# w_out turned by the host, the straight w_out narrowed in later blocks, and another order of the opening

## The chip, the cores and the metric

The kernel runs on one core of a Trainium2 chip. The metric is the device time of one execution in microseconds (us); lower is better. Engine names are those of the profile: PE multiplies matrices, PEld loads its weights, DVE and ACT do element-wise work, POOL is the general engine, SP issues loads and stores. Lines (L348) are those of the kernel before; in the change most lines stand some 60 to 85 further down, and its order rows carry its own numbers.

## The reference

```python
# 1. chunked attention: 4 x 8 heads, 768 tokens, head_dim 64; a chunk of 32 queries sees 56 keys and 8 memory keys
scores = scale * q_c @ k_full.T
a = exp(scores - max); a = a / (sum(a) + 1e-9); x = a @ v_full      # -> x (3072, 512)
# 2. a rational layer, w_in (512, 2048), w_out (2048, 512)
h = x @ w_in
g = (a0 + a1*h + a2*h**2 + a3*h**3) / (1 + |b0|*|h| + |b1|*h**2 + 1e-6)
x2 = g @ w_out
# 3. soft mixture: phi (512, 32), 8 experts of 4 slots, w1 (8, 512, 1024), w2 (8, 1024, 512)
logits = x2 @ phi
d = softmax over the tokens; c = softmax over the slots
slots = d.T @ x2;  y = relu(slots @ w1) @ w2 per expert;  out = c @ y
```

The weights w_in and w_out come as float64 (the draw makes them so); all else is float32.

## The kernel before

x2 is never formed. The logits are g @ (w_out @ phi): the 2048 x 32 product w_out @ phi is made once, in 16 tiles `wp`, and slots is (d.T @ g) @ w_out, with w_out needed as rows only at the very end.

The 3072 tokens are taken in 6 **blocks** of 512, and a block in 8 **steps** of 256 columns of h, 48 steps kk = 0 to 47. In a step PE makes h (`h_part`, L348), ACT and DVE the rational function (`run_step`: ACT L578, L579 and L581, then DVE L580, L590 and L591; ACT L595 and L596; POOL L556; DVE L603 and L604), PE turns the result (L374), and ACT copies it out of PSUM (L375). L578, which reads h, is the first operation of a step on ACT and is used below as its mark. Two h tiles exist in PSUM (`ps_h`); one comes free when L591 of its step has read it. Attention for two pairs of 128-token tiles of the next block runs between the steps, a slice at a time (`attention`, `slice_`). Block 0 multiplies in float32 with 8 matmuls a step; the later blocks use a split of x and w_in in two parts with 24 faster ones (`split_w`).

Float64 is narrowed on the chip (`f64_narrow`): a chunk of 128 x 1024 values comes as pairs of 32-bit words, and

```python
ACT.activation(lo, lo, AF.Copy, scale=LOW)                                   # L299
DVE.tensor_scalar(f, f, -F64_HI, F64_HI, ALU.max, ALU.min)                   # L300
ACT.activation(f, f, AF.Prelu, scale=2.0 ** -112, alpha=-(2.0 ** 32))        # L301
DVE.scalar_tensor_tensor(dst, hi, 3, lo, ALU.logical_shift_left, ALU.bitwise_or)   # L303
```

make 1024 float32 a row of it. There are 8 chunks of w_in (loads "i0" to "i7", L312) and 8 of w_out ("o0" to "o7", L317), all narrowed in the opening and in block 0, since block 0 uses a new chunk of w_in in every step and needs `wp` in its products with the logits. For a chunk of w_out, `narrow_w_out` also stores the float32 rows to a DRAM buffer `wo_dr` (POOL, L335), from where they come back at the end; `wp_chunk` turns them on PE (8 transposes, L447) and copies the two halves out, one on ACT (L451), one on DVE (L449); `wp_sum` multiplies by phi (L457, L462) and copies `wp` (L459, L463). The staging pool `p_g` has four buffers.

The order comes from the strings of `KN`. "loads" is the order of the first loads on SP: q, k and v of a pair of token tiles (q is 0.5 MB, k, v and a weight chunk 1 MB each), "c" the constants (three small loads, L266 to L268). "pre" orders the opening: A and B are the attention of the first two pairs of tiles, s, n and t narrow i0, o0 and i1, "f" are matmuls that only keep PE at work (`busy`, L284). "ord0", "ord" and "ordl" order a step of block 0, of blocks 1 to 4 and of block 5. In the opening the order on each engine is fixed by hand, but a scheduler may still put instructions of the part behind it between those; so the queue of an engine must be read, not the strings. The queues are served in order.

## Time and profile before

| what | us |
|---|---|
| median of 3 runs (582.21 to 582.49) | 582.41 |
| the profiled execution, device time | 583.87 |
| its span, first to last instruction | 582.1 |
| PE busy | 542.7 |
| DVE busy | 447.2 |
| ACT busy | 415.4 |
| POOL busy | 121.4 |

The profiled execution is 1.46 us above the median, and 1.8 us of it lie outside the span. Busy times are averages over stages that differ: the opening (0 to 39.84 us, where L578 first starts) is full of loads, block 0 lasts from there to 135.5 us, blocks 1 to 5 to about 500 us, and then come the experts with 32 MB of w1 and w2. Each stage is read by itself below.

### The profile page before, as it was taken

How to read it: one execution, taken by the hardware profiler on the slowest of the kernel's cores; microseconds unless marked ns; L12 is line 12 of the kernel's file. 1: busy time of each engine (PE TensorE's matmuls, PEld its weight loads, DVE VectorE, ACT ScalarE, POOL GpSimd, SP SyncE). 2: the span in 40 equal slices, each digit the busy share in tenths (PEclk: the TensorE clock that was granted, in tenths of full speed). 3: DMA queues.
4: the chain of work that ended last, by engine and by line, in shares of the span. 5: the costliest groups of instructions: out<-in, count | busy, mean ns of one | idle time of the engine just before them, and what ended most of it. 6: DMA issues, size and time to landing. Idle time of an engine off the chain costs nothing.

```text
span 582.1 us, 13606 instructions
## 1 busy us (share of the span) xinstructions
PE 542.7 (93%) x5910; PEld 369.7 (64%) x5910; DVE 447.2 (77%) x567; ACT 415.4 (71%) x542; POOL 121.4 (21%) x64
## 2 busy tenths in 40 slices
PE   6699999999999999999999999999999999899981
PEld 5554455457767777677766777767778577447351
DVE  4769999979998989878798798896987868821042
ACT  1489999888978878768887686877787869520132
POOL 0010322213221331313132222222132233100000
PEclk9799999999999999999999999999999999999996
DMA  8889874401135303231032111320374423989939
GB/s 354 353 333 384 306 258 193 144 37 48 62 110 182 110 7 103 75 110 73 2 109 74 62 59 64 109 75 1 109 272 163 144 78 142 393 309 377 411 138 358
DMA packets 21371, 97.41 MB, mean 167 GB/s; under 512 B 2624, under 2 KB 2752, under 8 KB 16320
## 3 DMA queue, kind: packets, MB, share of 16 engines
q1 hardware_dynamic: 20160, 92.35, 43.1%
q0 software_dynamic: 1152, 4.19, 1.8%
q8 instruction: 46, 0.75, 0.5%
q14 instruction: 13, 0.11, 0.1%
HBM read 86.05 MB, written 10.49 MB: 166 GB/s over the span
## 4 chain that ended last, share of the span: by engine, by line
PE 55%; DVE 14%; ACT 13%; DMA 9%; issue 3%; POOL 2%; SPq 0%; ACTq 0%; POOLq 0%; DVEq 0%
PE h L348 30%; PE m L374 5%; PE m L427 4%; PE lg L367 3%; ACT S L578 3%; DMA win<-in_moe_w_dram 3%; ACT S L579 3%; POOL S L556 2%; PE m L224 2%; DMA g<-in_moe_w_in_dram 2%; DMA g<-in_moe_w_out_dram 2%; DVE T L591 2%; ACT g L375 2%; DMA T<-in_moe_w_dram 2%; DVE S L580 2%
## 5 line engine op out<-in xcount | busy, mean ns | idle before, releaser
L348 PE MATMUL h<-xt,win 128*128 128x512 f32 x1024 | 269.9, 411 | 1.5 <-ACT xt L246 0.6
L348 PEld LDWEIGHTS h<-xt,win 128*128 128x128 f32 x1024 | 185.7, 188 | 48.1 <-issue 9.3
L556 POOL TENSOR_TENSOR S<-S,S 128x1024 f32<-128x1024 f32 x46 | 111.5, 2423 | 298.5 <-DVE S L580 298.5
L578 ACT ACTIVATE S<-h,ctab 128x1024 f32<-128x1024 f32 x47 | 52.4, 1114 | 50.2 <-PE h L348 48.9
L580 DVE SCALAR_TENSOR_TENSOR S<-S,S 128x1024 f32<-128x1024 f32 x47 | 57.4, 1222 | 37.6 <-ACT S L579 37.3
L590 DVE TENSOR_TENSOR T<-T,h 128x1024 f32<-128x1024 f32 x47 | 57.0, 1213 | 6.8 <-ACT T L581 6.6
L374 PEld LDWEIGHTS m<-ident,T 128*128 128x128 f32 x384 | 43.0, 141 | 29.5 <-issue 15.9
L591 DVE SCALAR_TENSOR_TENSOR T<-T,ctab,h 128x1024 f32<-128x1024 f32 x47 | 59.9, 1274 | 0.8
L603 DVE SCALAR_TENSOR_TENSOR T<-T,ctab,S 128x1024 f32<-128x1024 f32 x46 | 58.6, 1274 | 0.0
L604 DVE SCALAR_TENSOR_TENSOR T<-S,T 128x1024 f32<-128x1024 f32 x46 | 56.2, 1221 | 2.2
L581 ACT ACTIVATE T<-h,ctab 128x1024 f32<-128x1024 f32 x47 | 57.5, 1223 | 0.0
L375 ACT ACTIVATE g<-m 128x512 f32<-128x512 f32 x96 | 53.3, 601 | 3.2 <-PE m L374 2.9
L596 ACT ACTIVATE S<-S,ctab 128x1024 f32<-128x1024 f32 x47 | 54.4, 1158 | 0.9
L374 PE MATMUL m<-ident,T 128*128 128x128 f32 x384 | 52.6, 276 | 2.4 <-DVE a L185 1.4
L595 ACT ACTIVATE S<-S 128x1024 f32<-128x1024 f32 x47 | 50.4, 1073 | 6.0 <-DVE S L580 3.3
L579 ACT ACTIVATE S<-h,ctab 128x1024 f32<-128x1024 f32 x47 | 52.7, 1120 | 0.6 <-DVE T L603 0.6
L367 PE MATMUL lg<-T,wp 128*32 128x512 f32 x192 | 32.7, 605 | 1.3 <-DVE T L604 0.7
L348 PE MATMUL h<-xt,x 128*128 128x512 f32 x64 | 31.8, 608 | 0.0
L186 ACT ACTIVATE a<-a 128x512 f32<-128x512 f32 x22 | 13.6, 634 | 18.5 <-DVE a L185 18.5
L427 PE MATMUL m<-g,s 128*32 128x512 f32 x192 | 21.8, 595 | 0.4 <-ACT s L419 0.4
L335 POOL DMA_DIRECT2D wo<-win x8 | 5.8, 721 | 76.7 <-DVE win L303 67.9
L301 ACT ACTIVATE g<-g 128x1024 f32<-128x1024 f32 x16 | 18.6, 1173 | 3.0 <-DVE g L300 3.0
(193 smaller groups left out, 658.0 us busy)
## 6 DMA issues: line engine op xcount, KB each, us to landing
win<-in_moe_w_dram SPq DMA_DIRECT2D x32, 512.0 KB, 5.8
k<-in_kw_dram SPq DMA_DIRECT2D x11, 1024.0 KB, 8.0
v<-in_vw_dram SPq DMA_DIRECT2D x11, 1024.0 KB, 5.4
g<-in_moe_w_in_dram SPq DMA_DIRECT2D x8, 1024.0 KB, 7.6
g<-in_moe_w_out_dram SPq DMA_DIRECT2D x8, 1024.0 KB, 8.0
out_dram<-win SPq DMA_DIRECT2D x12, 512.0 KB, 5.0
q<-in_qw_dram SPq DMA_DIRECT2D x11, 512.0 KB, 3.6
wo<-win POOLq DMA_DIRECT2D x8, 512.0 KB, 7.0
```

The source lines that it names most:

```text
L348: PE.matmul(tile_[:, f2, :], lhsT=ww[:, c, f2 * P:f2 * P + P], rhs=xx[:, c, :], start=(n == 0), stop=(n == len(pairs) * NC - 1))
L374: st["turn"] = PE.transpose(pb[:, m, f2 * P:f2 * P + P], t_[:, f2, tt * P:tt * P + P], ident)
L375: ACT.activation(gts[b, qd][:, 2 * part:2 * part + 2, 2 * P * o:2 * P * o + 2 * P], pb, AF.Copy)
L556: POOL.tensor_tensor(out, q, w, ALU.mult)
L578: ACT.activation(s, hh, AF.Abs, scale=b0)
L579: ACT.activation(y, hh, AF.Square, scale=rb1)
L580: DVE.scalar_tensor_tensor(s, y, QC, s, ALU.add, ALU.add)
L581: ACT.activation(t, hh, AF.Identity, bias=a2, scale=a3)
L590: DVE.tensor_tensor(t, t, hh, ALU.mult)
L591: behind[kk] = DVE.scalar_tensor_tensor(t, t, a1, hh, ALU.add, ALU.mult).ins
L603: DVE.scalar_tensor_tensor(t, t, a0, w, ALU.add, ALU.mult)
L604: DVE.scalar_tensor_tensor(t, e, 2.0, t, ALU.subtract, ALU.mult, reverse0=True)
```

## The change

Five things change.

1. The host gives w_out a second time, turned (`w_turned`, float64, 8 chunks of 1 MB). Block 0 loads and narrows these in place of the straight ones ("o" and "n"), and `wp_sum` takes them as they are: `wp_chunk` with its transposes and copies is gone, and so are the stores to `wo_dr` in block 0.
2. The straight w_out is loaded and narrowed chunk by chunk in blocks 1 to 4 (`load_rows`, `narrow_rows`, "r" in "ord"): one chunk every three steps, from kk = 12 to 36, each with the four operations above and the store to `wo_dr`. Their buffers are the pool `p_x`, now 2 x 2048 in place of 4 x 1024 words a row.
3. The opening's attention takes each token tile by itself (`attention_first`), and the first h tile is made in two halves of 256 tokens, one after each pair (`h_first`; "H" and "J" are its two parts for pair 0 and pair 1).
4. The matmuls of `busy` are 512 columns long in place of 128, and there are 6 of them in place of 23.
5. The three loads of constants become one of 134 words a row, and the order strings are new. In a step of block 0, w_out is narrowed one chunk ahead in place of two.

```diff
-    'loads': "q0 q1 v0 i0 v1 c0 o0 i1 o1 q2 v2".split(),
-    'pre': "f10 A A f5 B B A A A A B B A A B B A A A A s B B B B A A f2 A B B A s A B B A f2 B s B B B c f4 n t n t t".split(),
-    'pre2': "i2 w0 z0 o2 n1 i3".split(),
-    'ord0': "at a1 w1 s2 h0 d1 at t o3 z1 i4 n2 at a2 y h1 p0 at p1 at at".split(),
-    'ord': "at a1 h0 d1 at t a2 y x2 h1 p0 p1 x1 at x3 at at".split(),
+    'loads': "q0 q1 v0 i0 v1 i1 c0 o0 q2 o1 v2".split(),
+    'pre': "f4 A A A A f2 A B A B B B A B B A A s B A A s A A A A H B B t t n B B n B B B B H J J c".split(),
+    'pre2': "i2 o2 i3".split(),
+    'ord0': "at a1 z0 s2 h0 d1 at t o3 i4 n1 at a2 y h1 p0 at p1 at at".split(),
+    'ord': "at a1 h0 d1 at t a2 y r x2 h1 p0 p1 x1 at x3 at at".split(),
...
+    def h_first(pair):
+        if 0 not in hs:
+            hs[0] = ps_h("h", [P, 2, BLK])
+        o = slice(P // 2 * pair, P // 2 * pair + P // 2)
+        x = xt[0][0].rearrange("p c (t r) -> p c t r", t=TT)
+        for f2 in range(2):
+            to = hs[0][:, f2, :].rearrange("p (t r) -> p t r", t=TT)
+            for c in range(NC):
+                PE.matmul(to[:, :, o], lhsT=w_f[0][:, c, f2 * P:f2 * P + P], rhs=x[:, c, :, o],
+                          start=(c == 0), stop=(c == NC - 1))
             yield
...
-        SP.dma_start(out=ctab[:, 0:4], in_=ca.unsqueeze(0).to_broadcast([P, 4]))
-        SP.dma_start(out=ctab[:, 4:6], in_=cb.unsqueeze(0).to_broadcast([P, 2]))
-        SP.dma_start(out=u_acc[:, 0:NC * NSLOT], in_=phi)
+        SP.dma_start(out=u_all[:, BLK - NC * NSLOT:BLK + 6], in_=cst)
...
-            PE.matmul(t, lhsT=ident, rhs=ident, start=True, stop=True)
+            PE.matmul(t, lhsT=ident, rhs=ident.unsqueeze(1).to_broadcast([P, 4, P]), start=True, stop=True)
...
-    def narrow_w_out(i):
-        f = scratch[i % 3].rearrange("p (j d) -> p j d", j=2)
-        yield from f64_narrow(f.bitcast(U32), stage_out.pop(i))
-        POOL.dma_start(out=wo_dr[i], in_=f)
-        wo[i] = f
+    def narrow_w_turned(i):
+        wos[i] = scratch[i % 3].rearrange("p (c f) -> p c f", c=NC)
+        yield from f64_narrow(wos[i].bitcast(U32), stage_out.pop(i))
+
+    def load_rows(i):
+        rows_of[i] = p_x("x", [P, 2, DM, 2], U32)
+        SP.dma_start(out=rows_of[i].rearrange("p c f w -> p c (f w)"), in_=w_out[i])
+
+    def narrow_rows(i):
+        src = rows_of.pop(i)
+        lo, hi = src[:, :, :, 0], src[:, :, :, 1]
+        ACT.activation(lo, lo, AF.Copy, scale=LOW)
+        f = hi.bitcast(F32)
+        DVE.tensor_scalar(f, f, -F64_HI, F64_HI, ALU.max, ALU.min)
+        yield
+        ACT.activation(f, f, AF.Prelu, scale=2.0 ** -112, alpha=-(2.0 ** 32))
+        t = p_x("x", [P, 2048])[:, 0:1024].rearrange("p (j d) -> p j d", j=2)
+        DVE.scalar_tensor_tensor(t.bitcast(U32), hi, 3, lo, ALU.logical_shift_left, ALU.bitwise_or)
+        POOL.dma_start(out=wo_dr[i], in_=t)
+        yield
...
-    def wp_chunk(i):
-        t = wo.pop(i)
-        ws = wos[i] = p_S("S", [P, 2, NC, P])
-        for j in range(2):
-            pb = bank([P, NC, P])
-            for c in range(NC):
-                PE.transpose(pb[:, c, :], t[:, j, c * P:c * P + P], ident)
-            if j:
-                DVE.tensor_copy(ws[:, j], pb)
-            else:
-                ACT.activation(ws[:, j], pb, AF.Copy)
...
+        elif what == "r":
+            n, m = divmod(kk - NSTEP - 4, 3)
+            if m != 1 and 0 <= n <= NSTEP:
+                with tc.issue_after(st["exp"]):
+                    if m == 2 and n < NSTEP:
+                        st["rows"] = narrow_rows(n)
+                        next(st["rows"])
+                    if m == 0 and n > 0:
+                        next(st["rows"])
+                    if m == 0 and n < NSTEP:
+                        load_rows(n)
```

How the queues stand at three places, with the program's own names. First SP, the ninth to the seventeenth load of the program. Before (g_163 is i1, g_161 and g_165 are o0 and o1, g_585 is i2; ctab and u take the constants):

```order
L266 DMA ctab_108<-in_moe_a_dram 128x4
L267 DMA ctab_108<-in_moe_b_dram 128x2
L268 DMA u_110<-in_moe_phi_dram 128x128
L317 DMA g_161<-in_moe_w_out_dram 128x2048
L312 DMA g_163<-in_moe_w_in_dram 128x2048
L317 DMA g_165<-in_moe_w_out_dram 128x2048
L128 DMA q_167<-in_qw_dram 128x1024
L129 DMA k_168<-in_kw_dram 128x2048
L135 DMA v_171<-in_vw_dram 128x2048
L312 DMA g_585<-in_moe_w_in_dram 128x2048
```

and now (g_157 is i1, g_160 and g_166 are the turned o0 and o1, g_560 is i2):

```order
L374 DMA g_157<-in_moe_w_in_dram 128x2048
L330 DMA u_109<-in_cst_dram 128x134
L379 DMA g_160<-in_w_turned_dram 128x2048
L128 DMA q_162<-in_qw_dram 128x1024
L129 DMA k_163<-in_kw_dram 128x2048
L379 DMA g_166<-in_w_turned_dram 128x2048
L135 DMA v_168<-in_vw_dram 128x2048
L374 DMA g_560<-in_moe_w_in_dram 128x2048
```

Before o1 now stand q and k of the third pair, and one load of constants in place of three.

Second ACT, around the copies of the transposed attention output into xt, which the first h waits for. Before (L246; m_541 and m_547 are those of pair 1, L299 and L301 the two ACT operations of a narrowing, L451 the copy of a turned w_out half, L578 the first operation of step 0):

```order
L246 ACTIVATE xt_143<-m_529 128x16x32
L299 ACTIVATE g_165<-g_165 128x1024
L246 ACTIVATE xt_143<-m_541 128x16x32
L246 ACTIVATE xt_143<-m_547 128x16x32
L271 ACTIVATE ctab_108<-ctab_108 128x2
L301 ACTIVATE g_165<-g_165 128x1024
```

and now (L297 is the copy into xt, m_528 and m_534 are pair 1; L361 and L363 the narrowing; L646 is what L578 was):

```order
L363 ACTIVATE g_157<-g_157 128x1024
L361 ACTIVATE g_160<-g_160 128x1024
L361 ACTIVATE g_166<-g_166 128x1024
L363 ACTIVATE g_160<-g_160 128x1024
L363 ACTIVATE g_166<-g_166 128x1024
L297 ACTIVATE xt_142<-m_528 128x16x32
L297 ACTIVATE xt_142<-m_534 128x16x32
L333 ACTIVATE u_109<-u_109 128x2
L336 ACTIVATE u_109<-u_109 128x1
L337 ACTIVATE u_109<-u_109 128x1
L361 ACTIVATE g_560<-g_560 128x1024
L363 ACTIVATE g_560<-g_560 128x1024
L646 ACTIVATE S_602<-h_446,u_109 128x1024
```

The copies of pair 1 stood behind one operation on o1; now they stand behind both, and behind the second one on o0. The narrowing of i2 now stands ahead of step 0.

Third ACT in blocks 1 to 4, between steps 17 and 18. Before (S_2562 is step 17, S_2695 step 18; L375 copies turned results, L383 the logits):

```order
L581 ACTIVATE T_2563<-h_2469,ctab_108 128x1024
L595 ACTIVATE S_2592<-S_2562 128x1024
L596 ACTIVATE S_2592<-S_2592,ctab_108 128x1024
L578 ACTIVATE S_2695<-h_2569,ctab_108 128x1024
L375 ACTIVATE g_2534<-m_2611 128x2x256
L375 ACTIVATE g_2534<-m_2617 128x2x256
L383 ACTIVATE s_11_2623<-lg_1981 128x512
```

and now (S_2434 is step 17, S_2569 step 18; L663 and L664 are what L595 and L596 were, L646 is L578, L457 is L375, L465 is L383, and L411 is the new first operation on a chunk of rows):

```order
L663 ACTIVATE S_2464<-S_2434 128x1024
L664 ACTIVATE S_2464<-S_2464,u_109 128x1024
L411 ACTIVATE x_2268<-x_2268 128x1024
L457 ACTIVATE g_2406<-m_2485 128x2x256
L457 ACTIVATE g_2406<-m_2491 128x2x256
L465 ACTIVATE s_11_2497<-lg_1843 128x512
L646 ACTIVATE S_2569<-h_2441,u_109 128x1024
```

The first operation of step 18 moved behind L411 and, here, behind three copies that followed it before. On DVE the clamp L413 of the same chunk and, in the next step, L417 stand between the operations of a step.

## Rows read from the trace of the kernel before

**Rows 1.** the page: busy us, share, instructions of each engine.

```profile
PE 542.7 (93%) x5910; PEld 369.7 (64%) x5910; DVE 447.2 (77%) x567; ACT 415.4 (71%) x542; POOL 121.4 (21%) x64
```

**Rows 2.** stretches: length, busy PE PEld DVE ACT POOL, PEclk, DMA share, GB/s.

```profile
0.00:39.84 39.84, 28.55 (x615) 22.33 (x616) 22.32 (x54) 17.57 (x26) 1.46 (x8) 0.91 0.87 344
39.84:135.50 95.66, 90.76 (x898) 49.01 (x897) 88.26 (x103) 87.13 (x112) 22.52 (x14) 1.00 0.59 216
...
174.10:412.20 238.10, 234.88 (x2818) 172.21 (x2817) 203.86 (x246) 185.49 (x237) 60.17 (x25) 1.00 0.24 80
```

**Rows 3.** the chain that ended last, up to 55 us: start, length, what.

```profile
3.06 13.62 DMA g<-in_moe_w_in_dram
...
16.70 12.81 DMA g<-in_moe_w_out_dram
...
29.53 1.20 ACT g L299
30.73 0.97 ACT xt L246 x2
...
31.74 7.13 PE h L348 x16
```

**Rows 4.** timeline of ACT, to 42 us: start, length, instruction [idle before <-releaser].

```profile
29.53 1.20 ACT L299 ACTIVATE g<-g 128x1024 uint32<-128x1024 uint32 x1 [0.58 <-DMA g<-in_moe_w_out_dram]
30.62 1.06 ACT L246 ACTIVATE xt<-m 128x512 f32<-128x512 f32 x2
...
39.34 0.60 ACT L451 ACTIVATE S<-m 128x512 f32<-128x512 f32 x1 [1.70 <-PE m L447]
39.84 1.11 ACT L578 ACTIVATE S<-h,ctab 128x1024 f32<-128x1024 f32 x1
```

**Rows 5.** the page: DMA issues, KB each, median us from issue to landing.

```profile
k<-in_kw_dram SPq DMA_DIRECT2D x11, 1024.0 KB, 8.0
...
q<-in_qw_dram SPq DMA_DIRECT2D x11, 512.0 KB, 3.6
```

**Rows 6.** stretches again, 16 to 22 us.

```profile
16.00:18.00 2.00, 0.79 (x56) 0.63 (x56) 1.90 (x5) 2.00 (x5) 0.00 (x0) 1.00 0.79 298
18.00:20.00 2.00, 0.09 (x8) 0.09 (x16) 1.93 (x6) 1.21 (x2) 0.00 (x0) 0.69 0.23 70
20.00:22.00 2.00, 2.00 (x76) 1.83 (x77) 1.86 (x7) 0.83 (x1) 0.00 (x0) 0.50 1.01 418
```

**Rows 7.** groups of ACT, 39.84 to 135.50 us: count | busy, mean ns | idle.

```profile
L299 ACT ACTIVATE g<-g 128x1024 uint32<-128x1024 uint32 x12 | 14.2, 1179 | 0.0
L301 ACT ACTIVATE g<-g 128x1024 f32<-128x1024 f32 x12 | 14.0, 1179 | 2.0 <-DVE g L300 2.0
...
L451 ACT ACTIVATE S<-m 128x512 f32<-128x512 f32 x8 | 4.8, 600 | 1.7 <-PE m L447 1.7
```

**Rows 8.** groups of PE, to 42 us.

```profile
L204 PE MATMUL m<-ident,T 128*128 128x128 f32 x8 | 2.0, 427 | 0.0
...
L204 PE MATMUL m<-ident,a 128*128 128x128 f32 x8 | 1.1, 280 | 0.0
```

**Rows 9.** groups of DVE, 39.84 to 135.50 us.

```profile
L303 DVE SCALAR_TENSOR_TENSOR win<-g 128x1024 uint32<-128x1024 uint32 x9 | 12.1, 1343 | 0.8 <-ACT g L301 0.8
...
L449 DVE COPY S<-m 128x512 f32<-128x512 f32 x8 | 5.5, 689 | 0.0
```

**Rows 10.** groups of PE, 39.84 to 135.50 us.

```profile
L447 PE MATMUL m<-ident,win 128*128 128x128 f32 x56 | 8.1, 280 | 1.6 <-DVE a L234 1.2 <-ACT S L451 0.4
```

**Rows 11.** the line L300, whole span: duration ns min/median/max.

```profile
L300 DVE TENSOR_SCALAR g<-g x16: 643/689/2278, 19.0 to 114.8; 128x1024 f32<-128x1024 f32 x16
```

**Rows 12.** waits, 174.10 to 412.20 us: total, times, longest.

```profile
ACT S L578 <- PE h L348: 34.8, 17, 2.5
DVE S L580 <- ACT S L579: 23.5, 16, 2.9
...
PEld h L348 <- DVE T L591: 1.6, 3, 0.8
```

## The prediction

> **What bounds the kernel now.** I began with the page: PE is busy 93% of the span, DVE and ACT 77% and 71% [rows 1]. That is an average, so I cut the span where its stages end. The table by stretches shows three different limits [rows 2]. The opening, 39.84 us, has PE busy for 28.55 us and the DMA engines for 0.87 of the time: it waits for loads. Block 0, 39.84 to 135.50, has PE at 90.76, DVE at 88.26 and ACT at 87.13 of 95.66 us: it is short of three engines at once. Steps 12 to 36 (174.10 to 412.20, those that the new narrowing falls into) have PE at 234.88 of 238.10 us, DVE at 203.86 and ACT at 185.49: PE sets the pace, with 3.2 us idle. Behind 500 us nothing changes, and that part starts earlier or later with what stands ahead.

> The chain that ended last shows what the opening waits for [rows 3]: the load of i0 (3.06 to 16.68), then that of o1, issued at 16.70 and landed at 29.51, ACT's L299 on it, the copies L246 of pair 1, and h (L348, 16 passes, 7.13 us). ACT's timeline says why a chunk that h does not need is in this chain: L299 on o1 stands ahead of L246 in ACT's queue and waits for the load, 0.58 us after the last work before it [rows 4]. L578 of step 0 follows at 39.84.

> **The change, part by part.** All counted against the profiled execution, 583.87 us; the median of the runs is 1.46 us lower.

> *The opening.* o1 still stands ahead of pair 1's copies, so its landing counts. Its load now has q and k of pair 2 ahead of it, 512 and 1024 KB [rows 5], which at the 418 GB/s of a full stretch [rows 6] take 3.76 us. Against that go the three small loads of constants. In the stretches 16:18 and 18:20 the loads move 298 and 70 GB/s in place of 418: 0.57 and 1.67 us lost, 2.24 together. A single load with rows of 134 words has no row of its own; 64 KB more at 418 GB/s are 0.16 us, and at worst nothing of the 2.24 is won. I take 2.1 won, as the nearest row is the full stretch right behind. So o1 lands at 29.51 + 3.76 - 2.1 = 31.2 (31.2 to 33.3).

> Behind it, ACT now does three operations of a narrowing (1.18 us each, [rows 7]) where L299 alone stood: 31.2 + 3.5 = 34.7. Two copies take 1.06 [rows 4]: 35.8. Of the h tile, the second half (pair 1) is left then: half of the first step's share. 16 passes took 7.13 us [rows 3], and a step has 8 float32 matmuls, or 16 passes; half of it is 3.6. [...] The halves of the tile save 3.6 us, and the later copies take them back.

> [...] Before, short matmuls (L284) kept PE at work up to the first h; the new strings have none behind pair 0's first softmax, and PE has nothing between pair 1's second product and o1's landing. From there come 8 transposes, 1.8 us of h for pair 0 and 3.6 for pair 1. [...] I take 1.6. [...]

> So L578 of step 0 comes at 41.0 in place of 39.84: **+1.2 us** (-0.4 to +5). Loads behind o1 (v, i2) follow at 2.5 us a chunk, i2 at about 36.2; its narrowing, now ahead of step 0 on ACT, ends by 38.6 and costs nothing as long as h is later than that.

> *Block 0.* Removed: 8 copies L451 on ACT (4.8 us, [rows 7]), 8 copies L449 on DVE (5.5, [rows 9]), 64 transposes on PE (56 of them 8.1 us in this stretch, [rows 10]). The issues of the stores to `wo_dr` go from POOL, which is 22.52 of 95.66 us busy [rows 2], so they are worth nothing. Also, at step 0 the opening has now narrowed five chunks (i0, i1, o0, o1, i2) in place of four: 2.4 us less of ACT, and of DVE one clamp, 0.69 [rows 11], and one L303, 1.34 [rows 9]. That is 7.2 us less on ACT, 7.5 on DVE, 8.1 on PE. ACT has the smallest, and one of its copies was done before 39.84: 6.6. As all three engines are over 91% busy, I take the whole of it: **-6.5 us** (-3 if their idle time grows as the load falls, -8.1 if PE alone counts). The step-later narrowing of w_out costs nothing: `wp` is needed by the products of step 1 at the earliest two steps on, and four staging buffers are filled as before.

> *Blocks 1 to 4.* Added: 8 chunks, each two ACT operations of 1.18 us, a clamp of 0.69 and an L303 of 1.34 on DVE; 18.9 us of ACT and 16.2 of DVE over 238 us. Both fit in their idle time (52.6 and 34.2 us, from [rows 2]), but not wherever they fall. An operation of ACT behind L596 delays the next step's L578, unless ACT would have waited there for PE: it did in 17 of 25 steps, 34.8 us in all [rows 12], so 2.0 us each, which covers 1.18. Of 16 insertions 8/25 meet no such wait: 5.1 x 1.18 = 6.0 us. L580 waited in 16 of 25 steps, 23.5 us in all [rows 12], 1.5 each: of 16 on DVE 5.8 meet none, mean 1.0, also 6. A late L578 or L580 makes L591 late, and that frees the h tile that PE wants; PE waited for it 3 times, 1.6 us in all [rows 12], so the two are near a tie and the slack is small. All hidden is 0; ACT's and DVE's in the same places is 6; in different ones 12. Ties on some steps only: I take half of 6, **+3.0 us**. The 8 new loads (8 MB) and 8 stores lie where the DMA engines are busy 0.24 of the time [rows 2]: nothing. The stores stand on POOL ahead of the next L556, which waits for a later operation of DVE anyway: nothing.

> Sum: +1.2 - 6.5 + 3.0 = -2.3; 583.87 - 2.3 = 581.6 for an execution like the profiled one, and **580.1** beside the median of 582.41.

> **The rivals.**
> *The rows hide entirely.* Then the third term is 0: 577.1. For it: ACT and DVE have 52.6 and 34.2 us idle. Against it: [rows 12], the 8 and 9 steps without a wait.
> *ACT and DVE become the bound in steps 12 to 36.* Insertions in steps without a wait stall PE, on both engines in different places for two thirds of the 12 us: +8 in place of +3, so 585.1. It decides as soon as the third term passes 5.3. For it: PE has only 3.2 us idle to catch up with. This is the case on the slow side.
> [...]
> *The opening doesn't wait for o1.* If the queue order did not matter, h would follow v of pair 1, some 5 us earlier (first term -4): 574.9. The order on ACT speaks against it.

> **Chances.** The forecast (-4 to -1.2) 0.42, hidden rows (beyond -4) 0.22, ACT and DVE as the bound 0.20, the slow first h 0.12, an early opening 0.04. The range takes the hidden rows with a good opening, 582.41 - 6.9 = 575.5, and on the other side the bound case short of its last microsecond, 584.5. A change of under 0.2% (1.2 us) cannot be told from none here. Faster by more: forecast, hidden rows and early opening, less a part of the forecast, 0.62. Slower by more: the bound case and a part of the slow h, 0.22. The rest, 0.16, lies between.

> **What would show it.** ACT's first operation on o1 waits for its load at about 31 us, and pair 1's copies stand behind it. The first operation of step 0 starts near 41, that of step 8 near 130 in place of 135.5. PE's idle time in steps 12 to 36 grows from 3.2 us by about 3. It is wrong if the rows add no idle time to PE, if block 0 keeps its 95.7 us with the copies gone, or if step 0 starts before 38 or behind 44.

## The result, and the profile after

The changed kernel is slower: 588.43 us (median of 20 runs, 581.44 to 593.32) against 582.37 us of the kernel before (20 runs on the same chip, 581.70 to 584.54). The ratio is 1.0079, with a 95% interval of 1.0059 to 1.0099; it is that of the fast runs, without six of the changed kernel that lie over 1.5% above its fastest, while the medians as they stand give 1.0104. Forecast were 580.1 us and a range of 575.5 to 584.5. The changed kernel's runs lie 12 us apart, those of before 3 us; that spread will matter below.

The profiled execution took 587.72 us (span 585.9). In the changed kernel's line numbers L646 is the first operation of a step (L578 before), L431 is h (L348), L215 and L159 are the small matmuls of attention, and L411, L413, L415 and L417 are the four operations on a chunk of rows, L406 its load and L418 its store.

The opening, ACT in time (start, length, instruction, idle time before it), as in [rows 4]:

```profile
31.12 1.17 ACT L361 ACTIVATE g<-g 128x1024 uint32<-128x1024 uint32 x1 [3.62 <-DMA g<-in_w_turned_dram]
32.17 2.19 ACT L363 ACTIVATE g<-g 128x1024 f32<-128x1024 f32 x2
34.25 1.07 ACT L297 ACTIVATE xt<-m 128x512 f32<-128x512 f32 x2
...
40.22 1.12 ACT L646 ACTIVATE S<-h,u 128x1024 f32<-128x1024 f32 x1 [1.73 <-PE h L311]
```

ACT waits for o1 until 31.12, the copies of pair 1 stand behind it, and step 0 begins at 40.22 (39.84 before). The stretches around it, and the three that answer to [rows 2], with a fourth for the tail (length, busy PE, PEld, DVE, ACT, POOL, granted clock, DMA share, GB/s):

```profile
32.00:34.00 2.00, 1.53 (x7) 1.53 (x8) 1.65 (x3) 2.00 (x3) 0.00 (x0) 0.51 1.01 410
34.00:36.00 2.00, 2.00 (x9) 1.70 (x8) 0.74 (x2) 1.75 (x6) 0.00 (x0) 0.64 1.00 418
36.00:38.00 2.00, 2.00 (x11) 1.77 (x10) 1.14 (x4) 1.90 (x3) 0.00 (x0) 1.00 1.01 393
...
0.00:40.22 40.22, 30.57 (x600) 21.44 (x608) 22.86 (x49) 19.33 (x26) 0.74 (x7) 0.83 0.94 381
40.22:128.10 87.88, 84.42 (x836) 43.41 (x839) 82.41 (x93) 81.30 (x103) 16.69 (x7) 1.00 0.45 169
168.00:415.00 247.00, 237.77 (x2818) 172.98 (x2817) 217.62 (x260) 202.10 (x253) 64.38 (x32) 0.99 0.34 118
442.40:585.90 143.50, 122.48 (x876) 78.45 (x874) 70.54 (x94) 70.22 (x99) 20.40 (x10) 0.96 0.67 253
```

Block 0 took 87.88 us in place of 95.66: that gain came, and more than was forecast. Steps 12 to 36 took 247.0 in place of 238.1, with PE idle for 9.2 us in place of 3.2; PE's busy time rose as well, from 234.9 to 237.8 with as many matmuls. Cut at steps 8 and 40, the profiled executions differ like this: opening +0.4, block 0 -7.8, steps 8 to 40 (314.3 against 303.9) +10.4, tail +0.8; together +3.8, which is 587.72 less 583.87. So what has to be explained is +10.4 where +3.0 was forecast. The tail's +0.8 was not followed up.

Two rows of the waits in 168 to 415 us (total, times, longest) stand out beside [rows 12]:

```profile
DVE x L413 <- DMA x<-in_moe_w_out_dram: 3.9, 3, 1.7
PE m L215 <- issue: 3.1, 1, 3.1
```

The first is a clamp that waits for its load. The second is one stop of 3.1 us in front of a small matmul for which the profile names no releaser. Its place, in PE's timeline:

```profile
383.33 0.65 PE L215 MATMUL m<-v,a 64*32 64x64 f32 x32
383.91 0.98 PE L431 MATMUL h<-xt,win 128*128 128x512 f32 x3
384.82 1.26 PE L215 MATMUL m<-v,a 64*32 64x64 f32 x80
389.22 0.35 PE L215 MATMUL m<-v,a 64*32 64x64 f32 x16 [3.14 <-issue]
389.50 0.43 PE L499 MATMUL m<-ident,s 32*128 32x32 f32 x4
389.86 4.15 PE L431 MATMUL h<-xt,win 128*128 128x512 f32 x10
```

and in stretches:

```profile
384.00:386.00 2.00, 2.00 (x83) 1.45 (x84) 2.00 (x4) 2.00 (x5) 2.00 (x1) 1.00 0.92 330
386.00:388.00 2.00, 0.08 (x7) 0.00 (x0) 1.78 (x2) 1.39 (x2) 0.29 (x1) 1.00 0.35 137
388.00:390.00 2.00, 0.78 (x21) 0.65 (x21) 0.36 (x1) 0.04 (x1) 0.00 (x0) 1.00 0.00 0
390.00:392.00 2.00, 2.00 (x6) 1.62 (x7) 2.00 (x4) 0.24 (x1) 0.00 (x0) 0.61 0.49 135
392.00:394.00 2.00, 2.00 (x9) 1.07 (x12) 0.67 (x2) 0.00 (x0) 0.00 (x0) 0.54 0.92 389
```

PE stops in the middle of a group of 128 like instructions, 16 before its end, while a load and a store of rows (380.3 to 387.5) keep the DMA engines busy, 0.83 to 0.92 of the time in 382:386. Behind the stop the granted clock is at 0.61 and 0.54 in the two stretches of 390:394. Step 34 took 15.0 us; 10.1 would have done, as will be seen.

### The profile page after: what moved, and what is told of

It is laid out like the page before. It is cut to its first block, busy times and chain, and to the rows that moved or that the text cites. A ratio compares the mean times of both kernels' runs of the same rounds, so it can differ in the third digit from the quotient of the medians.

```text
span 585.9 us, 13442 instructions
## 1 busy us (share of the span) xinstructions
PE 542.1 (93%) x5828; PEld 364.4 (62%) x5828; DVE 457.0 (78%) x568; ACT 428.1 (73%) x550; POOL 119.7 (20%) x64
## 4 chain that ended last, share of the span: by engine, by line
PE 48%; DVE 20%; ACT 12%; DMA 11%; issue 5%; POOL 2%; SPq 0%; ACTq 0%; DVEq 0%; POOLq 0%
PE h L431 24%; PE m L456 4%; PE lg L449 3%; ACT S L646 3%; DMA win<-in_moe_w_dram 3%; DVE T L658 3%; DVE T L659 3%; PE m L509 2%; DVE T L671 2%; DMA g<-in_w_turned_dram 2%; DMA g<-in_moe_w_in_dram 2%; ACT S L647 2%; PE m L215 2%; DVE S L648 2%; DMA T<-in_moe_w_dram 2%
## 5 line engine op out<-in xcount | busy, mean ns | idle before, releaser
L431 PE MATMUL h<-xt,win 128*128 128x512 f32 x1008 | 263.7, 410 | 1.4 <-DVE T L659 1.1
L431 PEld LDWEIGHTS h<-xt,win 128*128 128x128 f32 x1008 | 183.8, 189 | 47.8 <-issue 8.5
L646 ACT ACTIVATE S<-h,u 128x1024 f32<-128x1024 f32 x47 | 52.6, 1118 | 46.1 <-PE h L431 42.9
L659 DVE SCALAR_TENSOR_TENSOR T<-T,u,h 128x1024 f32<-128x1024 f32 x47 | 59.8, 1271 | 0.7
L671 DVE SCALAR_TENSOR_TENSOR T<-T,u,S 128x1024 f32<-128x1024 f32 x46 | 58.4, 1270 | 0.0
L649 ACT ACTIVATE T<-h,u 128x1024 f32<-128x1024 f32 x47 | 57.6, 1227 | 0.0
L457 ACT ACTIVATE g<-m 128x512 f32<-128x512 f32 x96 | 53.2, 604 | 3.1 <-PE m L456 2.8
L664 ACT ACTIVATE S<-S,u 128x1024 f32<-128x1024 f32 x47 | 54.5, 1159 | 1.0
L663 ACT ACTIVATE S<-S 128x1024 f32<-128x1024 f32 x47 | 50.5, 1075 | 4.4 <-DVE S L648 4.4
L647 ACT ACTIVATE S<-h,u 128x1024 f32<-128x1024 f32 x47 | 52.8, 1123 | 0.0
L449 PE MATMUL lg<-T,wp 128*32 128x512 f32 x192 | 34.2, 605 | 1.3 <-DVE T L672 0.7
L431 PE MATMUL h<-xt,x 128*128 128x512 f32 x64 | 31.3, 611 | 1.1 <-DVE x L365 1.1
L215 PE MATMUL m<-v,a 64*32 64x64 f32 x1280 | 19.2, 223 | 3.5 <-issue 3.1
L215 PEld LDWEIGHTS m<-v,a 64*32 64x32 f32 x1280 | 16.0, 105 | 9.1 <-issue 4.3
L361 ACT ACTIVATE g<-g 128x1024 uint32<-128x1024 uint32 x16 | 18.7, 1167 | 3.6 <-DMA g<-in_w_turned_dram 3.6
```

The lines of the kernel that those rows point to most:

```text
L431: PE.matmul(tile_[:, f2, :], lhsT=ww[:, c, f2 * P:f2 * P + P], rhs=xx[:, c, :], start=(n == 0), stop=(n == len(pairs) * NC - 1))
L646: ACT.activation(s, hh, AF.Abs, scale=b0)
L647: ACT.activation(y, hh, AF.Square, scale=rb1)
L649: ACT.activation(t, hh, AF.Identity, bias=a2, scale=a3)
L659: behind[kk] = DVE.scalar_tensor_tensor(t, t, a1, hh, ALU.add, ALU.mult).ins
L664: st["exp"] = ACT.activation(w, w, AF.Exp, bias=ex_b, scale=-1.0).ins
```

## The experiments

All medians are compared with the kernel before on the same chip, whose median was 582.58 to 582.75 us each time, and the ratios with their intervals are to it. Two theories were tried first. Theory B in the expectations is the prediction's own: operations of the rows on ACT and DVE delay the h tiles. Theory A, its rival, is that the transfers hold up PE's instructions where it runs many small matmuls.

**1. Without rows** (blocks 1 to 4 as before; the turned chunk is stored in block 0 in place of the straight one).

```diff
-    'ord': "at a1 h0 d1 at t a2 y r x2 h1 p0 p1 x1 at x3 at at".split(),
+    'ord': "at a1 h0 d1 at t a2 y x2 h1 p0 p1 x1 at x3 at at".split(),
```

> The change without the narrowing of the straight w_out in blocks 1 to 4; the turned chunks are stored in block 0 instead, so the expert part works on a wrong w_out. Step 0 and block 0 as in the change (step 8 near 128 us). Both theories put the loss into the rows: steps 8 to 40 should take about 304 us as before the change in place of 314, and the whole 577 (575 to 579). If it stays above 584, the loss is elsewhere in the change.

Measured: 578.36 us (577.80 to 578.92), ratio 0.9923 [0.9908, 0.9938]. The whole loss against the changed kernel without them, 10.1 us, is in the rows. Steps 8 to 40 took 305.3 us, still 1.4 more than before the change, of which 1.1 lie in step 8.

**2. Transfers without the operations.** `narrow_rows` keeps only its store; the loads take rows of w1.

> The eight 1 MB loads and 0.5 MB stores stay at the steps of the change, the ACT and DVE operations on them are left out (the loads bring rows of w1, so the end is computed from other data). Theory A, the transfers hold up PE's instructions where it runs many small matmuls: 583 to 589, with a spread of several us from run to run, and idle times of PE of 2 to 3 us in front of small matmuls that nothing in the profile releases. Theory B, the operations on ACT and DVE delay the h tiles: 577 (575 to 579), spread under 2 us.

Measured: 583.82 us (580.33 to 586.69), ratio 1.0015 [0.9992, 1.0038]. Inconclusive: with nothing to hold them, all eight loads and stores were issued between 168 and 224 us, and the stores on POOL waited 24.3 us for their loads with the step's own multiply behind them. It is not the change's traffic; experiment 5 mends it.

**3. Operations without transfers.** One chunk is loaded, the four operations run eight times on it, and nothing is stored in later blocks.

> All eight chunks' ACT and DVE operations stay in blocks 1 to 4 but work on one chunk that is loaded once; no further loads and no stores there (the turned chunks are stored in block 0, so the end is computed from other data). Theory A: 577 to 580, spread under 2 us. Theory B: 584 to 589, PE idle in front of h and of the turned results released by DVE.

Measured: 580.52 us (578.50 to 580.87), ratio 0.9957 [0.9940, 0.9973]: 2.2 us above the run without rows. The size of the forecast's +3.0 for the operations was about right, and 8 us are still missing.

**4. The rows at other steps.** Second halves, stores and loads go to the steps 14, 18, 22, 26, 30, 34, 36 and 38, first halves to 13, 16, 20, 24, 28, 32, 35 and 37.

> The change with the rows at other steps: second half of a chunk at steps 14, 18, 22, 26, 30, 34, 36, 38 and the next load and the store right behind it, first half one or two steps ahead, so that the transfers lie mostly in steps without the many small matmuls of attention and the operations mostly in steps where ACT waited for PE. Theory A: 578 to 581 and a spread under 2 us. Theory B: 580 to 585, as only part of the operations find room. If neither holds, 588 as the change.

Measured: 582.64 us (581.60 to 584.06), ratio 0.9995 [0.9983, 1.0007]. It lies in the range of Theory B and above that of A, but operations and transfers both moved, so it does not tell them apart. The same work at other steps is 5.8 us faster than the changed kernel, and the runs lie 2.5 us apart. So the place decides, not the amount.

**5. Transfers at the change's own steps**, with the four operations on 8 columns.

```diff
-        lo, hi = src[:, :, :, 0], src[:, :, :, 1]
+        lo, f = src[:, 0:8], src[:, 8:16]
...
-        DVE.scalar_tensor_tensor(t.bitcast(U32), hi, 3, lo, ALU.logical_shift_left, ALU.bitwise_or)
+        DVE.tensor_tensor(t[:, 0, 0:8], f, lo, ALU.add)
         POOL.dma_start(out=wo_dr[i], in_=t)
```

> The eight chunks of rows are loaded and stored at the same steps as in the changed kernel, and the clamp, the prelu and the two other operations stand in their places, but on 8 columns instead of 1024 (the loads take 1 MB of w1 and the stores write a constant, so the second halves multiply by other numbers than the reference's). Before: 582.4; without rows 578.4; operations alone 580.5; the changed kernel 588.4. If the transfers themselves cost (the DMA engines fill, and the PE stalls beside them), this run is near 578.4 + 8 = 586. If it is the long operations meeting late loads (a clamp that waits for its chunk with DVE's other work behind it, and then takes 1.1 us), the wait stays and the work goes: near 582. If the transfers are free, as predicted: 579.

Measured: 580.22 us (578.61 to 580.72), ratio 0.9951 [0.9935, 0.9966]. Not the 586 of the transfer theory: alone the transfers cost 1.9 us, as the operations alone cost 2.2.

**6. Loads and operations, no stores of rows** (the store's line is out; the turned chunk is stored as in experiment 1).

> The changed kernel without the eight stores of rows in blocks 1 to 4 (in their place the turned chunk is stored in block 0, which are wrong numbers for the second halves of the later blocks); loads and all operations stay. If the loads cost (the clamp waits for its chunk, 3.9 us of waiting in three steps, and the small matmuls stall while a load runs): 586 to 588, as the changed kernel. If the stores cost (4 MB written from POOL's queue): near the operations alone, 580.5. If either alone is harmless and only both at once fill the DMA engines: 581 to 582.

Measured: 583.14 us (581.41 to 585.41), ratio 1.0004 [0.9990, 1.0018]. None of the three forecasts: between that for loads that cost by themselves and that for both at once.

**7. Stores and operations, one load.**

> The changed kernel with one load of rows only, at step 12; the operations run eight times on that chunk and all eight stores stay at their steps (so all chunks but one hold other numbers). The counterpart of the run without stores: if the loads cost, this one is near the operations alone, 580.5 to 581.5; if the stores cost, 586 to 588.

Measured: 578.97 us (578.27 to 580.26), ratio 0.9935 [0.9919, 0.9950]. Stores without loads cost nothing that shows; the time is even 1.5 us below the operations alone, and that difference was not explained.

**8. Stores from SP.**

```diff
-        POOL.dma_start(out=wo_dr[i], in_=t)
+        SP.dma_start(out=wo_dr[i], in_=t)
```

> The changed kernel with its eight stores issued by SP, on the queue of the loads, instead of by POOL; nothing else changed. POOL's queue then holds no store that waits for the last of the four operations (24.0 us of waiting in 7 steps), but on SP every load behind the store waits with it. If the store's place on POOL cost (the work behind it on POOL, or POOL's way of issuing): about 584 or less. If the loads cost: no change, 588. If loads behind the waiting store come late: over 590.

Measured: 583.10 us (579.08 to 586.50), ratio 1.0001 [0.9973, 1.0029]. Of the twelve runs six lie at 579.1 to 581.7 and six at 584.5 to 586.5, and none between: as if one event of 5 us happens or not. The median is as forecast for a cost of the stores' place on POOL, but a median between two clusters decides little. The profiled execution is one of the lower six, and has no stop in front of L215.

Taken together, 6 to 8 said that loads are needed for the loss, stores make it worse, and that it comes in pieces of 5 us. The lengths of single steps in the profiled executions, from one first operation to the next (L646 and its like), show where:

```
kernel                    step 12  17+18    28  33+34   8 to 40
before                       10.7   19.5  10.7   20.3     303.9
without rows                 10.7   19.4  10.7   20.3     305.3
transfers, 8 columns         10.7   20.8  11.8   20.3     306.9
operations, one load         12.4   19.5  10.7   20.8     307.3
stores, one load             12.4   19.5  10.7   20.4     307.0
stores from SP               12.4   20.5  10.7   20.5     307.9
loads, no stores             12.4   20.5  12.4   21.5     310.5
changed                      12.4   20.5  12.4   25.5     314.3
even steps (9)               12.4   19.8  10.7   20.9     309.5
odd steps (10)               12.4   20.5  12.4   25.8     318.3
combined (11)                12.4   20.1  10.7   21.4     309.4
page shift (12)              12.4   20.5  12.4   20.5     309.4
```

Against the run without rows, steps 12 and 28 cost 1.7 us each and come from the clamp (below). The large one, 5.3 us, is steps 33 and 34 with the stop. In the changed kernel the transfers of four rounds (issued at steps 15, 21, 27 and 33) run beside small matmuls, and the other rounds do not. That gave the next pair.

**9. Those four rounds one step later.**

```diff
-            n, m = divmod(kk - NSTEP - 4, 3)
...
+            first, second = (14, 17, 20, 23, 26, 29, 32, 35), (16, 18, 22, 24, 28, 30, 34, 36)
```

> The changed kernel with the four rounds of store and load that its table puts at steps 15, 21, 27 and 33 put one step later, at 16, 22, 28 and 34 (first halves and the other four rounds stay). In the trace of the changed kernel exactly these four run beside the attention's small matmuls (L159 or L215), and in step 34 TensorE stood for 3.14 us in the middle of such a group. If small matmuls beside a transfer of rows are what costs: no such stop, 588.4 falls to 581 to 583, and the runs lie within 3 us instead of 12. If the cost is late loads and full ACT and DVE: 586 to 588, since the operations are the same.

Measured: 582.66 us (580.94 to 588.84), ratio 1.0004 [0.9981, 1.0028]. The stop of step 34 shrank to 0.40 us. The median is as forecast; the spread is not (3 us were forecast), since one of twelve runs was at 588.84 and the others lie 4 us apart.

**10. The mirror: all rounds beside small matmuls.** `first` is 14, 18, 20, 24, 26, 30, 32, 34 and `second` 15, 19, 21, 25, 27, 31, 33, 35.

> The mirror of the run above: the four rounds that the changed kernel has at steps 18, 24, 30 and 36 are moved to 19, 25, 31 and 35, so that all eight transfers lie beside small matmuls (first halves at 14, 18, 20, 24, 26, 30, 32 and 34). If the small matmuls beside a transfer cost: 590 to 595, with runs as far apart as those of the changed kernel or further. If not: 586 to 589, or what the changed places of the operations give.

Measured: 591.91 us (591.30 to 592.72), ratio 1.0155 [1.0138, 1.0173]. The time is as forecast; the spread of its four runs, 1.4 us, is not. The same operations and bytes, at steps shifted by one, give 582.66 or 591.91; the operations moved with the transfers, so this pair alone does not part them.

**11. A combined version**: the even steps, the stores from SP, and the narrowing of o1 by hand behind pair 1's copies.

```diff
-    'pre': "f4 ... H J J c".split(),
+    'pre': "f4 ... H J J c m m".split(),
...
+            "s": narrow_w_in(0), "n": narrow_w_turned(0), "m": narrow_w_turned(1), "t": narrow_w_in(1), "c": constants()}
```

> The run with the rounds at even steps, with two more edits: the stores of rows are issued by SP instead of POOL, and in the opening the narrowing of the second turned chunk stands by hand behind the copies of pair 1, so that step 0 begins 2 us earlier. Without rows 578.4; the wait and the slow clamp in step 12 add 1.7, steps 17 and 18 add 1.1, the opening gives back 1 to 2: 579 to 580.5, below before (582.4) by 0.3 to 0.6 per cent and below the changed kernel by 1.4. If the opening does not give (o1's data come late and the narrowing holds ACT): 581 to 582.

Measured: 580.34 us (579.48 to 582.27), ratio 0.9963 [0.9949, 0.9978]: faster than both kernels. In ACT's timeline the copies no longer wait for o1, and step 0 begins 1.9 us earlier than in the changed kernel:

```profile
30.57 1.26 ACT L297 ACTIVATE xt<-m 128x512 f32<-128x512 f32 x2 [0.17 <-PE m L295]
...
38.28 1.10 ACT L646 ACTIVATE S<-h,u 128x1024 f32<-128x1024 f32 x1
```

**What the stop is.** The page's list of DMA queues has a line for instructions; it is the same before and after:

```profile
q8 instruction: 46, 0.75, 0.5%
```

46 packets of 16,384 bytes, and PE and PEld have 11,747 records in the changed kernel with those of their queue: 255 to a packet. By that count they are taken here for PE's own instructions on their way to it, and experiment 12 bears that out. Around the stop of the changed kernel, the queues of 383 to 387 us, and then of the half microsecond behind:

```profile
DMA packets 252, 1.29 MB, mean 322 GB/s; under 512 B 31, under 2 KB 31, under 8 KB 159
## 3 DMA queue, kind: packets, MB, share of 16 engines
q1 hardware_dynamic: 109, 0.76, 54.8%
q0 software_dynamic: 143, 0.52, 32.3%
...
q8 instruction: 1, 0.02, 11.6%
q0 software_dynamic: 1, 0.00, 0.1%
```

In the first window there are only rows; the instructions come at 387.03 and have landed at 387.96, and PE goes on 1.26 us later. Now PE's records (its queue's and PEld's with them) ahead of each stop of 0.3 us or more that PE has with "issue" as its releaser, counted in the traces: 449, 705 and 961 in the kernel before (at 13.4, 19.9 and 26.6 us), 449 and 8897 in the changed one, 449 and 7617 with transfers on 8 columns, 8897 in experiments 6, 9, 10 and 11 as well, and 9409 a second time in 10. (449 is in every kernel, in the opening.) Every one of them is 193 above a multiple of 256. So these stops all lie at the same place of such a count by 256, which is read here as the border between one packet of instructions and the next.

How late a packet was, from the traces: the time from the earliest record of PE at which this packet began in any of ten of these kernels, to its begin in this one (us):

```
packet      without rows  stores from SP  even steps  changed  odd steps
18                  -0.2             1.3         0.0      4.1        3.8
23                   0.1             1.1         0.0      3.8        4.2
24                   0.1             2.1        -0.0      4.0        3.6
28                  -0.1             0.1         0.1      0.2       -0.1
33                   0.1             0.5         3.9      7.3        7.6
record at 33        8624            8626        8688     8897       8897
```

Packets 18, 23, 24 and 33 were due while a load and a store of rows of the changed kernel ran, or 0.6 us ahead (33). When they were due, PE still had 120 to 280 records to go to the border, and three of the packets came in time; packet 33 met a group of small matmuls, which spends 256 records, matmuls and weight loads, in 1.9 us (at the pace of 96 matmuls in 1.41 us, below). If this is the cause, it must be possible to move the stop without touching a transfer or an operation.

**12. The same program, PE's list shifted by some 110 instructions.**

```diff
-    'pre': "f4 A A A A f2 A B ...".split(),
+    'pre': "g28 f3 A A A A f2 A B ...".split(),
...
+        for _ in range(n):
+            PE.matmul(t[0:32, 0, 0:32], lhsT=ident[0:32, 0:32], rhs=ident[0:32, 0:32], start=True, stop=True)
```

> The changed kernel with 28 tiny matmuls (32x32) in place of one of the four idle matmuls at the very start: TensorE's list of instructions grows by some 110 ahead of everything else, and not one transfer, operation or wait behind that is altered. In the traces TensorE's instructions arrive in pieces of 16 KB (queue 8, kind instruction, 46 of them, some 256 records of TensorE to each); in the changed kernel and in the run with all rounds at odd steps the piece with number 33 came 7 us late beside a transfer of rows, and TensorE stopped behind the very same record, the 8897th. If late pieces beside the transfers are the cost, the borders of all pieces now lie some 110 records earlier, piece 33 is asked for about 8 us before the transfer of step 34, the stop there goes, and the time falls to 582 to 585 (the transfers alone with their operations were 583.1). If small matmuls beside a transfer are slow wherever the borders lie (contention for data): unchanged, 587 to 590.

Measured: 584.27 us (582.83 to 585.96), ratio 1.0021 [1.0007, 1.0034]: 4.2 us faster than the changed kernel, with runs 3 us apart. The stop in step 34 is gone (20.5 us for steps 33 and 34), and every other step from 8 to 40 is as long as in the changed kernel to 0.1 us. The same group runs through beside the same transfers (PE's timeline, and the stretch beside it):

```profile
388.56 0.96 PE L436 MATMUL h<-xt,win 128*128 128x512 f32 x3
389.45 1.41 PE L215 MATMUL m<-v,a 64*32 64x64 f32 x96
...
388.00:390.00 2.00, 2.00 (x68) 1.45 (x67) 1.96 (x5) 2.00 (x7) 1.44 (x1) 1.00 0.90 332
390.00:392.00 2.00, 2.00 (x80) 1.74 (x73) 2.00 (x3) 1.97 (x3) 0.95 (x1) 1.00 0.95 307
```

So it is not that small matmuls are slow beside a transfer. But there is a new stop, in the opening, where the DMA engines are full:

```profile
30.06 1.43 PE L283 MATMUL h<-S,T 64*32 64x64 f32 x122
35.08 0.43 PE L283 MATMUL h<-S,T 64*32 64x64 f32 x6 [3.58 <-issue]
```

It stands at record 1217, again 193 above a multiple of 256; its packet ran from 32.60 to 33.70. Step 0 began at 44.95 in place of 40.22. In the profiled executions (585.96 and 587.72 us) step 34 gives 4.9 us and the opening takes 4.7 back; which of these stops the other runs had is not known, so the price of the stop in step 34 is read from the step, and not from the medians.

## Why the prediction was wrong

*What bounds the kernel.* The three limits were read rightly, and the two parts that argue from them came out.

*The opening, +1.2 us: right in its steps.* o1 landed at 31.1 (31.2 forecast), pair 1's copies began at 34.25 (34.7), and step 0 at 40.22 (41.0): +0.4. o1 came 1.6 us later than the 29.51 of before, as the sum of q and k of pair 2 less the small loads had it; the two terms were not measured apart. The 41.0 is 35.8 for the copies, 3.6 for half of h and 1.6 for a slower h; no run shows the 1.6 us by themselves. In the changed kernel step 0 began 4.9 us behind the end of the copies (35.32), 1.3 more than the 3.6, and the granted clock was 0.51 and 0.64 in 32:36 and 1.00 in 36:38. Experiment 11 confirms that o1 stood in the way: 1.9 us.

*Block 0, -6.5 us: right, and low.* It fell by 7.8, near the -8.1 of PE alone. The run without rows gives the first two terms by themselves: 578.36, where the rival "the rows hide entirely" had 577.1. In its profiled execution steps 8 to 40 became 1.4 us longer, 1.1 of them in step 8, right behind the shorter block 0; this was not followed up.

*Operations in blocks 1 to 4, +3.0: near in size (2.2 alone), but in part by luck.* The prediction had them spread over the steps without a wait, through an L591 that is late and frees the h tile late. In the profiled execution of experiment 3, 1.7 of the 2.0 us by which steps 8 to 40 are longer than without rows are step 12 alone, the clamp beside POOL's multiply (below), and the waits of PE for that operation of DVE did not grow in it (0.9 us, and 1.5 without rows). In the changed kernel the path of the prediction does show once, 1.1 us in steps 17 and 18 (L659 is what L591 was), and these are longer in the kernels that load a chunk at step 15 (20.5 to 20.8) than in those with one load (19.5):

```profile
PE h L431 <- DVE T L659: 1.1, 1, 1.1
```

*The step that failed* is one sentence: "The 8 new loads (8 MB) and 8 stores lie where the DMA engines are busy 0.24 of the time [rows 2]: nothing." The share of 0.24 was a mean. A load and its store take about 7 us (380.3 to 387.5 for those of step 33), with the engines nearly full (0.83 to 0.92 in 382:386 of the changed kernel), and two things that wait for DMA fall into those 7 us:

- PE's instructions. This is shown for the stop in step 34: all stops lie on packet borders, 193 records above a multiple of 256, and this one goes when the border moves while every transfer and operation stays (experiment 12). The time also goes with the share of transfers that lie beside small matmuls (582.66, 588.43 and 591.91 us for the even steps, the change and the odd steps), though the operations moved with them there. How much of the packet's lateness is the transfers' is said below. One stop with the low clock behind it costs 4.9 us (15.0 against 10.1 for step 34). The two clusters of experiment 8, 5 us apart, fit one such stop that comes in half of the runs; which stops the other runs had was not profiled.
- The clamp L413. In step 12 it waits 0.54 us for its load and then takes 2.55 us, 2.00 of them beside a multiply of POOL, where the median of [rows 11] is 0.69, so most of it is put down to POOL and not to DMA; behind it in DVE's queue stands L180 of attention, and PE waits 1.26 us for that. The step is 1.7 us longer in every kernel with a clamp of full width, and not longer with 8 columns. In step 28 it waits 1.74 us for its load, and the step is again 1.7 us longer, without stores too (experiment 6); where the clamp came later in DVE's order, at 334.1 us in experiment 8, the step kept its 10.7 us. From the timelines of DVE, POOL and PE:

```profile
172.36 2.55 DVE L413 TENSOR_SCALAR x<-x 128x1024 f32<-128x1024 f32 x1 [0.54 <-DMA x<-in_moe_w_out_dram]
174.83 1.21 DVE L658 TENSOR_TENSOR T<-T,h 128x1024 f32<-128x1024 f32 x1
...
326.74 1.36 DVE L413 TENSOR_SCALAR x<-x 128x1024 f32<-128x1024 f32 x1 [1.74 <-DMA x<-in_moe_w_out_dram]
```

```profile
171.97 2.39 POOL L624 TENSOR_TENSOR S<-S,S 128x1024 f32<-128x1024 f32 x1 [7.97 <-DVE S L648]
```

```profile
179.89 0.63 PE L456 MATMUL m<-ident,T 128*128 128x128 f32 x4 [1.26 <-DVE a L180]
```

From the run without rows to the changed kernel, steps 8 to 40 grew by 9.1 us: step 12 1.7, steps 17 and 18 1.1, step 28 1.7, steps 33 and 34 5.3 with the stop, less 0.7 in the others. That closes the sum for the profiled execution; the runs of the changed kernel lie up to 5.6 us above and 6.3 us below it, and their stops were not seen.

*The rivals.* "ACT and DVE become the bound" had a time nearer the result (585.1), but not the cause: with the operations alone the kernel is at 580.5. None of the four that were given a chance was about transfers. Yet the kernel before showed such stops three times in its opening, in front of small matmuls, the first and the third with the DMA engines full, the second with a DMA share of 0.23 in 18:20 [rows 6] (PE's timeline of before):

```profile
13.42 0.85 PE L164 MATMUL h<-xt,xt 64*32 64x64 f32 x64 [1.92 <-issue]
19.91 1.34 PE L224 MATMUL h<-v,a 64*32 64x64 f32 x72 [2.19 <-issue]
26.62 1.11 PE L224 MATMUL h<-S,T 64*32 64x64 f32 x89 [0.95 <-issue]
```

The prediction read the stretch of the second one, in [rows 6], for the rate of the loads alone. A rival "PE's instructions come late beside the new transfers", at 2 us a stop (from the second of these rows) and with one to four of the rounds beside small matmuls, would have reached from 580.1 to 582 to 588.

*What stays open.* Transfers make packets late: packets 18 and 23, due 1 to 3 us behind the start of a load of rows, were 3.4 to 4.2 us late in the changed kernel and in experiments 5 and 10, and -0.2 to 0.5 us in experiments 1, 3, 4, 9 and 11, which have no transfer of rows there. But transfers are not the only thing that makes a packet late, and packet 33 is such a case. In experiments 9 and 11 it was 3.9 and 4.5 us late with no transfer of rows near it and the DMA engines idle (0, 8 and 0 GB/s in the three stretches of 380:386 of experiment 9), and in experiment 3, which has no load of rows after the first, 4.6 us; the stops were then 0.40, 0.95 and 0.17 us. In experiments 5 and 8, with a load and a store that began 0.0 and 0.6 us behind the time at which it was due, it was in time (-0.1 and 0.5 us). So some 4 to 5 of the changed kernel's 7.3 us may be of that other kind, and the transfers, which the packet then met, would have added some 3 (an estimate from these runs); what asks for a packet, and when, the traces do not tell. Nor was it tried to keep the operations and put the transfers elsewhere in a step, since the issue follows the buffers.

## What to carry to other kernels

A mean DMA share tells nothing of the microseconds in which a transfer runs (0.24 over steps 12 to 36 before, 0.83 to 0.92 beside a load and a store here): lay the new transfers over PE's timeline, and look first for what arrives by DMA there, PE's instructions included. Groups of many tiny matmuls were the place where a late packet of instructions showed; an idle time before a small matmul with "issue" as its releaser was the sign, longest beside nearly full DMA engines (3.14 to 3.58 us), and counting PE's records up to it (193 above a multiple of 256 each time here) pointed to the cause. Transfers that have slack should be issued right behind such a group, so that they have landed before the next; the same bytes and operations one step earlier or later were worth 9 us here.
